# Attention, routed experts and a gated layer on one core: vector arithmetic off GpSimd, another weight decode, Silu, and a written-out plan

## The chip, the core and the metric

One core of a Trainium2 chip runs the whole program in one launch. The metric is the device time in microseconds (us) of that launch, the median of several runs. A core has five engines, each with its own in-order list of instructions: TensorE (PE in the rows; PEld is its weight load), VectorE (DVE), ScalarE (ACT), GpSimd (POOL) and SyncE (SP), which here only issues DMAs. The engines work side by side and wait for each other through semaphores.

## The reference

Three layers on float32 data, the last layer's weights being float64:

```python
# attention: B=4, H=8, S=768, D=48, a state of 48x48 per batch and head
k_n = k / (norm(k) + 1e-6)
for t in range(S):
    y[t]  = q[t] @ state
    v_old = state.T @ k_n[t]
    state = state + beta[t] * outer(k_n[t], v[t] - v_old)
# experts: x is [3072, 384]; tokens with x @ w_skip > 0 go to one of 8 experts
e = argmax(x @ w_gate); gate = softmax(x @ w_gate)[e]
x = x + gate * (relu(x @ w1[e]) @ w2[e])           # w1 384x1024, w2 1024x384
# gated layer
xn  = x / sqrt(mean(x*x) + 1e-6) * rms_g
g   = xn @ w_gate2;  val = xn @ w_val               # 384x1536 each
out = (g * sigmoid(g) * val) @ w_out                # 1536x384
```

## The kernel before

Every float32 product is made of three float16 products: both sides are split into a rounded half "hi" and the rest "lo", and hi.hi, lo.hi and hi.lo are added up in PSUM (`mm3`, lines 296 to 298). So nearly every tensor has a conversion to hi (`conv`, lines 269 to 271, on VectorE or ScalarE) and a subtraction for lo (`tt`, line 277, or `stt`, line 279).

**Attention** runs in six groups g of 128 tokens, each of two halves (chunks of 64 tokens) and of two pairs of batches. For a group: the K tiles are loaded, squared and summed (`norms`), scaled (`kn`), split (`kh`, `kl`), transposed by DMA (`trk`), and multiplied with themselves (`gramk`); the grams go to DRAM and come back with one 32x32 block on each partition (`lda`). `solve` inverts 128 such triangular blocks at once on VectorE: 30 steps, each a multiply (`sm`) and an add (`sa`) of j x (31-j) elements, 60 instructions that depend on each other. Its result is scaled by a mask (`bm`, `Ts`), split in two orders (`Th`, `Tl`), stored, loaded again; `merge` joins 32-blocks to 64-blocks. `prepq` makes the masked q-k products (`pm`, split to `ph`, `pl`), and `step` runs the recurrence of one chunk. Each finished tile is routed (`Route`) and scattered to its expert's rows by indirect DMAs on GpSimd (line 645).

**Experts.** Eight experts one after the other: weights loaded and split (`wh`, `wl`), 256 rows loaded, split, transposed, 64 matmul groups `m1` with relu and lo halves (`relu`, `hl`), then `m2` and a store. Beside them 27 pieces of the gated layer's float64 weights are **decoded** to float32 and split (lines 700 to 709). The buffers of this stage lie over those of attention's that are used up.

**Gated layer.** Groups of 1, 1, 2, 4, 4, 4, 4, 4 tiles of 128 tokens: load, gather the expert's result by an indirect DMA on GpSimd (line 764), add, norm (`sq2`, the root with one Newton step), scale by 1/rms and by rms_g (`xn`), split, transpose; then 12 column blocks of two products `gv`, sigmoid (line 793), times g (`silu`), times val (`gh`), split (`ghh`, `ghl`); then `mo` (lines 804 to 806), copy and store.

**The order.** The kernel does not emit these operations in program order. `Sched.op` records each with the engines that may do it and an estimated cost; `balance` and the tables ORDER, ENGINES and URGENT choose engines and priorities by (stage, tag, group); `run` plays the program through with these costs and picks slots; `emit` writes the lists. In ENGINES a number says how many operations of a tag go to the last engine that may do them: for `kl` 8, 0, 8, 2, 8, 7 of 8 in the six groups on GpSimd, for `kn` 2, 4, 4, 1, 4, 0 of 4, for `pl` 8 of 8, for `gbl` all, for `Ts` in three groups, for `decl` 8, 9, 9 of 9 and for `decm` 9, 6, 8 of 9; `bm` has GpSimd alone. All DMAs but the indirect ones go through SP's list.

## Time and profile before

| | before |
|---|---|
| runs, us | 1086.28, 1085.55, 1086.11 (median 1086.11) |
| profiled execution, span from first to last instruction | 1071.0 us |
| median of the runs less that span | 15.1 us |
| busy in the span: TensorE, VectorE, ScalarE, GpSimd | 821.9, 767.7, 444.5, 298.9 us |
| instructions: VectorE, ScalarE, GpSimd | 1558, 818, 257 |
| mean granted TensorE clock | 0.870 of 2.4 GHz |

Of the profiled execution the page gives the span; what lies around it (launch and end) is in the runs' times alone. A group of instructions in the profile is named by the line of the helper that emitted it, so `kl`, `pl`, `sm` and many others all stand at line 277 and are told apart by engine and shape. "busy" is the union of a group's instructions, "mean" that of one instruction; consecutive instructions of an engine overlap a little in the records. An engine's idle time is put down to what released it last.

### The profile page before, as it was taken

How to read it: one execution, taken by the hardware profiler on the slowest of the kernel's cores; microseconds unless marked ns; L12 is line 12 of the kernel's file. 1: busy time of each engine (PE TensorE's matmuls, PEld its weight loads, DVE VectorE, ACT ScalarE, POOL GpSimd, SP SyncE). 2: the span in 40 equal slices, each digit the busy share in tenths (PEclk: the TensorE clock that was granted, in tenths of full speed). 3: DMA queues.
4: the chain of work that ended last, by engine and by line, in shares of the span. 5: the costliest groups of instructions: out<-in, count | busy, mean ns of one | idle time of the engine just before them, and what ended most of it. 6: DMA issues, size and time to landing. Idle time of an engine off the chain costs nothing. (4 is left out here: it accounts for less than half of the span.)

```text
span 1071.0 us, 23370 instructions
## 1 busy us (share of the span) xinstructions
PE 821.9 (77%) x9590; PEld 568.3 (53%) x9590; DVE 767.7 (72%) x1558; ACT 444.5 (42%) x818; POOL 298.9 (28%) x257
## 2 busy tenths in 40 slices
PE   0440776867667677279898629999999999999996
PEld 0440665756656566267566329754554445445463
DVE  6697998989888888999999999877505651441500
ACT  2230674856657586254535134555202321221200
POOL 7540354335354334421331454330000000000000
PEclk9665687768869697589999859999999999999999
DMA  6985779797998869589776362460210110000000
GB/s 222 212 180 90 165 168 166 209 159 166 187 160 203 165 147 268 186 221 304 217 228 218 127 170 74 119 155 8 37 38 1 30 30 16 15 1 30 1 31 32
DMA packets 307619, 137.94 MB, mean 129 GB/s; under 512 B 273022, under 2 KB 289107, under 8 KB 307506
## 3 DMA queue, kind: packets, MB, share of 16 engines
q1 hardware_dynamic: 304434, 129.32, 50.1%
q0 software_dynamic: 3072, 7.07, 2.3%
q8 instruction: 77, 1.26, 0.5%
q14 instruction: 36, 0.29, 0.1%
HBM read 77.38 MB, written 33.03 MB: 103 GB/s over the span
## 5 line engine op out<-in xcount | busy, mean ns | idle before, releaser
L296 PE MATMUL bank<-arena 128*128 128x64 f16 (+5 forms) x2096 | 381.0, 243 | 158.9 <-DMA arena<-arena 107.3
L277 POOL TENSOR_TENSOR arena<-arena 64x512 f16<-64x512 f32 (+9 forms) x175 | 229.5, 1316 | 574.4 <-ACT arena L269 356.5
L297 PE MATMUL bank<-arena 128*128 128x64 f16 (+5 forms) x2096 | 380.7, 243 | 4.1 <-DVE arena L279 2.1
L298 PE MATMUL bank<-arena 128*128 128x64 f16 (+5 forms) x2096 | 380.0, 243 | 2.1 <-ACT arena L269 2.0
L277 DVE TENSOR_TENSOR arena<-arena 128x512 f16<-128x512 f32 (+22 forms) x503 | 261.1, 523 | 74.6 <-ACT arena L269 59.5
L269 ACT ACTIVATE arena<-arena 128x512 f16<-128x512 f32 (+8 forms) x272 | 194.2, 723 | 239.0 <-DVE arena L279 101.4
L296 PEld LDWEIGHTS <-arena 128*128 128x128 f16 x2096 | 204.9, 105 | 151.7 <-DMA arena<-arena 55.8
L297 PEld LDWEIGHTS <-arena 128*128 128x128 f16 x2096 | 203.7, 104 | 120.5 <-issue 68.6
L269 ACT ACTIVATE arena<-bank 128x384 f16<-128x384 f32 (+4 forms) x286 | 142.2, 520 | 217.2 <-PE bank L806 105.6
L298 PEld LDWEIGHTS <-arena 128*128 128x128 f16 x2096 | 203.6, 104 | 45.9
L279 DVE SCALAR_TENSOR_TENSOR arena<-arena 128x768 f16<-128x768 f32 (+3 forms) x160 | 145.0, 926 | 8.6 <-ACT arena L269 3.5
L277 DVE TENSOR_TENSOR arena<-bank,arena 128x512 f32<-128x512 f32 (+2 forms) x120 | 68.0, 578 | 55.0 <-ACT arena L793 52.5
L806 PE MATMUL bank<-arena 128*128 128x384 f16 x288 | 93.9, 326 | 0.0
L804 PE MATMUL bank<-arena 128*128 128x384 f16 x288 | 93.9, 326 | 0.0
L805 PE MATMUL bank<-arena 128*128 128x384 f16 x288 | 93.9, 326 | 0.0
L279 DVE SCALAR_TENSOR_TENSOR arena<-arena,bank 128x512 f32<-128x512 f32 (+2 forms) x96 | 51.9, 547 | 45.0 <-PE bank L298 44.9
L793 ACT ACTIVATE arena<-bank 128x512 f32<-128x512 f32 (+2 forms) x96 | 45.1, 486 | 74.9 <-PE bank L298 74.6
L747 PE MATMUL bank<-arena 128*128 128x384 f16 x128 | 43.6, 340 | 11.3 <-ACT arena L269 6.1
L270 DVE CAST arena<-arena 64x384 f16<-64x384 f32 (+6 forms) x64 | 33.9, 533 | 21.6 <-PE bank L805 10.7
L302 PE MATMUL bank<-arena 128*128 128x48 f16 x544 | 43.3, 196 | 5.5 <-ACT arena L269 3.8
L306 PE MATMUL bank<-arena 128*128 128x48 f16 x544 | 27.5, 194 | 25.1 <-DVE arena L279 24.2
L749 PE MATMUL bank<-arena 128*128 128x384 f16 x128 | 43.6, 340 | 1.1 <-DVE arena L279 1.1
(107 smaller groups left out, 859.4 us busy)
## 6 DMA issues: line engine op xcount, KB each, us to landing
arena<-in_w_dram SPq DMA_DIRECT2D x24, 512.0 KB, 7.8
arena<-in_w_dram SPq DMA_DIRECT2D x32, 384.0 KB, 4.7
arena<-in_qv_dram SPq DMA_DIRECT2D x12, 768.0 KB, 5.3
gd<-arena SPq DMA_DIRECT2D x12, 512.0 KB, 2.8
arena<-in_kn_dram SPq DMA_DIRECT2D x12, 384.0 KB, 4.3
arena<-gd SPq DMA_DIRECT2D x36, 128.0 KB, 3.1
xd<-arena SPq DMA_DIRECT2D x12, 384.0 KB, 2.9
arena<-in_wg_dram SPq DMA_DIRECT2D x9, 512.0 KB, 4.8
```

The lines of the kernel that those rows point to most:

```text
L269: if e is s.nc.scalar: e.activation(out(),in_(),AF.Copy,scale=scale)
L277: return s.sch.op(alts,lambda e: e.tensor_tensor(out(),a(),b(),op=op),r=r,w=w,tag=tag,prio=prio)
L279: return s.sch.op([("DVE",0.07+n*0.00104)],lambda e: e.scalar_tensor_tensor(out(),a(),sc() if callable(sc) else sc,b(),op0=op0,op1=op1),r= ...
L296: nc.tensor.matmul(out,lh,rh,start=first,stop=False,skip_group_check=True)
L297: nc.tensor.matmul(out,ll,rh,start=False,stop=False,skip_group_check=True)
L298: nc.tensor.matmul(out,lh,rl,start=False,stop=last,skip_group_check=True)
L747: nc.tensor.matmul(py.ap,hT.ap[:,f,0,bs],w.ap[:,0,c],start=f==0,stop=False)
L749: nc.tensor.matmul(py.ap,hT.ap[:,f,1,bs],w.ap[:,0,c],start=False,stop=f==7)
L793: s.act(lambda e,sg=sg,pp=pp: e.activation(sg.ap,pp[0].ap,AF.Sigmoid,scale=2.0**-7),T,[pp[0]],[sg],table="sig",tag="sig")
L804: nc.tensor.matmul(po.ap,hT.ap[:,f,0,bs],s.wo.ap[:,0,c],start=f==0,stop=False)
L805: nc.tensor.matmul(po.ap,hT.ap[:,f,0,bs],s.wo.ap[:,1,c],start=False,stop=False)
L806: nc.tensor.matmul(po.ap,hT.ap[:,f,1,bs],s.wo.ap[:,0,c],start=False,stop=f==11)
```

## The change

- GpSimd keeps the constants, six clears of buffers, and the 48 indirect DMAs. Every `tensor_tensor` goes to VectorE, and so does `bm`.
- The decode clamps the float64 exponent by a maximum (`LEAST`) where it multiplied with a mask; the multiply is gone.
- rms_g is one number for each row of w_gate and w_val. It multiplies the hi and lo halves in the decode (`scale=g`), the normalised tokens lose their scaling by it, and the split of x takes 1/rms as its scale directly, so that `xn` and its buffer are gone.
- ScalarE's Silu takes the place of Sigmoid; the multiply by g is gone.
- ORDER, ENGINES, URGENT and the code that plays the program through are gone. A plan stands in the file instead: the order of all 3630 operations, the engine of each (a digit) and the slot of each of 1627 buffers; `follow` reads it. By its digits VectorE gets 1608 operations, ScalarE 755, GpSimd 66. 24 of the 27 decode pieces are ahead of the first `x2` in VectorE's list; of 48 `kh` 36 are on ScalarE; of 24 `gs` 7 are on VectorE.

The comments are taken out too. The number of slots in each pool stays, but for the decode's temporaries (four for six).

```diff
-    def tt(s,out,a,b,op,n,r,w,engs="DP",tag="",prio=0.0):
-        alts=[]
-        if "D" in engs: alts.append(("DVE",0.07+n*0.00104))
-        if "P" in engs: alts.append(("POOL",0.13+n*0.00194))
+    def tt(s,out,a,b,op,n,r,w,port=1,tag="",prio=0.0):
+        alts=[("DVE",0.07+n*0.00104,port)]
...
+    def follow(s,plan):
+        order,engines,slots=plan
+        for o,e in zip(s.ops,engines): o.eng=ENGINES[int(e)]; o.start=o.end=0.0
+        for b,i in zip(s.bufs,slots): b.slot=i
+        s.order=[s.ops[i] for i in order]
...
-        s.tt(lambda: bm.ap,lambda: s.c.m32.ap,lambda: btg().unsqueeze(2).to_broadcast([128,32,32]),ALU.mult,1024,[bt,s.c.m32],[bm],engs="P")
+        s.tt(lambda: bm.ap,lambda: s.c.m32.ap,lambda: btg().unsqueeze(2).to_broadcast([128,32,32]),ALU.mult,1024,[bt,s.c.m32],[bm])
...
-                t=s.pdt.buf([512],U32); u=s.pdt.buf([512],U32); m=s.pdt.buf([512],F32)
+                t=s.pdt.buf([512],U32); u=s.pdt.buf([512],U32)
+                rs=[] if sc else [s.rg]; g=(lambda sc=sc: sc) if sc else (lambda j=j: s.rg.ap[:,j//3:j//3+1])
                 D(lambda e,t=t,lo=lo: e.tensor_scalar(t.ap,lo(),29,None,op0=ALU.logical_shift_right),[raw],[t],0.34)
-                D(lambda e,t=t,u=u,hi=hi: e.scalar_tensor_tensor(u.ap,hi(),3,t.ap,op0=ALU.logical_shift_left,op1=ALU.bitwise_or),[raw,t],[u])
+                D(lambda e,u=u,hi=hi: e.tensor_scalar(u.ap,hi(),0x7FFFFFFF,None,op0=ALU.bitwise_and),[raw],[u],0.34)
+                D(lambda e,u=u: e.tensor_scalar(u.ap.bitcast(F32),u.ap.bitcast(F32),LEAST,None,op0=ALU.max),[u],[u],0.34)
+                D(lambda e,t=t,u=u: e.scalar_tensor_tensor(u.ap,u.ap,3,t.ap,op0=ALU.logical_shift_left,op1=ALU.bitwise_or),[u,t],[u])
                 D(lambda e,t=t,hi=hi: e.tensor_scalar(t.ap,hi(),0xC0000000,None,op0=ALU.bitwise_and),[raw],[t],0.34)
                 D(lambda e,t=t,u=u: e.scalar_tensor_tensor(u.ap,u.ap,0x3FFFFFFF,t.ap,op0=ALU.bitwise_and,op1=ALU.bitwise_or),[u,t],[u])
-                D(lambda e,t=t,hi=hi: e.tensor_scalar(t.ap,hi(),0x7FFFFFFF,None,op0=ALU.bitwise_and),[raw],[t],0.34)
-                D(lambda e,t=t,m=m,sc=sc: e.tensor_scalar(m.ap,t.ap.bitcast(F32),2.0**-15,sc,op0=ALU.is_ge,op1=ALU.mult),[t],[m],0.34)
-                s.tt(lambda m=m: m.ap,lambda u=u: u.ap.bitcast(F32),lambda m=m: m.ap,ALU.mult,512,[u,m],[m],tag="decm")
-                s.conv(lambda dst=dst,cs=cs: dst.ap[:,0,cs],lambda m=m: m.ap,512,[m],[(dst,(j,0))],tag="dech")
-                s.tt(lambda dst=dst,cs=cs: dst.ap[:,1,cs],lambda m=m: m.ap,lambda dst=dst,cs=cs: dst.ap[:,0,cs],ALU.subtract,512,[m,(dst,(j,0))],[(dst,(j,1))],tag="decl")
+                s.conv(lambda dst=dst,cs=cs: dst.ap[:,0,cs],lambda u=u: u.ap.bitcast(F32),512,[u]+rs,[(dst,(j,0))],scale=g,tag="dech")
+                s.stt(lambda dst=dst,cs=cs: dst.ap[:,1,cs],lambda u=u: u.ap.bitcast(F32),g,lambda dst=dst,cs=cs: dst.ap[:,0,cs],ALU.subtract,512,[u,(dst,(j,0))]+rs,[(dst,(j,1))],tag="decl")
...
-                s.stt(lambda xn=xn: xn.ap,lambda x=x,b=b: x.ap[:,b],lambda ri=ri,b=b: ri.ap[:,b:b+1],lambda: s.rg.ap,ALU.mult,DM,[(x,b),ri,s.rg],[xn],tag="xn")
-                s.conv(lambda xh=xh: xh.ap[:,0],lambda xn=xn: xn.ap,DM,[xn],[(xh,0)],scale=8.0,tag="xnh")
+                s.conv(lambda xh=xh: xh.ap[:,0],lambda x=x,b=b: x.ap[:,b],DM,[(x,b),ri],[(xh,0)],scale=rb,tag="xnh")
...
-                s.act(lambda e,sg=sg,pp=pp: e.activation(sg.ap,pp[0].ap,AF.Sigmoid,scale=2.0**-7),T,[pp[0]],[sg],table="sig",tag="sig")
-                s.tt(lambda sg=sg: sg.ap,lambda pp=pp: pp[0].ap,lambda sg=sg: sg.ap,ALU.mult,T,[pp[0],sg],[sg],engs="D",tag="silu")
+                s.act(lambda e,sg=sg,pp=pp: e.activation(sg.ap,pp[0].ap,AF.Silu,scale=2.0**-7),T,[pp[0]],[sg],table="silu",tag="silu")
...
-        sch.order_by,sch.engines,sch.urgent=ORDER,ENGINES,URGENT
-        sch.run(verbose)
+        sch.follow(PLAN)
```

## Rows read from the trace of the kernel before

**Rows 1.** The windows: length, busy time (instructions) of each engine, clock, DMA share, GB/s.
```profile
0.00:100.00 100.00, 25.68 (x504) 24.84 (x504) 73.13 (x133) 23.62 (x34) 47.73 (x59) 0.73 0.73 178
...
200.00:300.00 100.00, 67.06 (x1567) 60.85 (x1565) 91.09 (x218) 63.86 (x107) 44.63 (x35) 0.79 0.89 175
...
0.00:440.00 440.00, 263.45 (x6033) 234.99 (x6034) 371.12 (x818) 241.77 (x410) 192.77 (x166) 0.76 0.82 180
440.00:612.00 172.00, 134.48 (x965) 96.11 (x965) 167.37 (x270) 72.33 (x134) 54.33 (x40) 0.90 0.72 217
612.00:637.00 25.00, 0.91 (x9) 0.91 (x9) 23.86 (x49) 7.25 (x17) 15.04 (x13) 0.58 0.56 158
637.00:707.00 70.00, 68.67 (x750) 56.91 (x749) 61.60 (x179) 36.51 (x106) 29.43 (x33) 0.98 0.52 124
707.00:1062.00 355.00, 354.41 (x1837) 179.37 (x1834) 143.78 (x246) 86.29 (x154) 7.37 (x7) 1.00 0.09 25
...
```

**Rows 2.** The page's costliest groups: GpSimd, line 277, all forms together.
```profile
...
L277 POOL TENSOR_TENSOR arena<-arena 64x512 f16<-64x512 f32 (+9 forms) x175 | 229.5, 1316 | 574.4 <-ACT arena L269 356.5
...
```

**Rows 3.** Groups by shape, VectorE, whole span: count | busy us, mean ns | idle.
```profile
...
L279 DVE SCALAR_TENSOR_TENSOR arena<-arena 128x768 f16<-128x768 f32 x64 | 67.8, 1067 | 3.6 <-ACT arena L269 3.5
...
L277 DVE TENSOR_TENSOR arena<-bank,arena 128x512 f32<-128x512 f32 x84 | 57.2, 687 | 52.3 <-ACT arena L793 49.9 <-PE bank L298 1.1 <-POOL arena L277 0.8
...
L277 DVE TENSOR_TENSOR arena<-arena 128x512 f16<-128x512 f32 x59 | 40.3, 690 | 59.4 <-ACT arena L269 59.0
...
L279 DVE SCALAR_TENSOR_TENSOR arena<-bank,arena 128x256 f16<-128x256 f32 x64 | 25.3, 413 | 0.0
...
L277 DVE TENSOR_TENSOR arena<-arena 128x220 f32<-128x220 f32 x24 | 14.6, 610 | 0.6
...
L277 DVE TENSOR_TENSOR arena<-arena 64x384 f16<-64x384 f32 x15 | 9.0, 598 | 0.3
...
L277 DVE TENSOR_TENSOR arena<-arena 128x84 f32<-128x84 f32 x24 | 8.3, 346 | 0.6
...
```

**Rows 4.** Groups by shape, VectorE, 564.2 to 583 us, while GpSimd computes nothing.
```profile
...
L279 DVE SCALAR_TENSOR_TENSOR arena<-arena 128x768 f16<-128x768 f32 x8 | 7.5, 948 | 0.0
...
L702 DVE SCALAR_TENSOR_TENSOR arena<-arena 128x512 uint32<-128x512 uint32 x1 | 0.7, 684 | 0.0
...
L703 DVE TENSOR_SCALAR arena<-arena 128x512 uint32<-128x512 uint32 x1 | 0.4, 427 | 0.0
...
```

**Rows 5.** Groups by shape, VectorE, 440 to 612 us, the experts.
```profile
...
L702 DVE SCALAR_TENSOR_TENSOR arena<-arena 128x512 uint32<-128x512 uint32 x21 | 24.9, 1185 | 0.5
...
```

**Rows 6.** Groups by shape, VectorE, 90.2 to 108.9 us, while GpSimd computes nothing.
```profile
...
L277 DVE TENSOR_TENSOR arena<-arena 128x1024 f32<-128x1024 f32 x1 | 1.2, 1224 | 4.8 <-DMA arena<-gd 4.8
...
L277 DVE TENSOR_TENSOR arena<-arena 128x84 f32<-128x84 f32 x2 | 0.5, 246 | 0.1
...
L277 DVE TENSOR_TENSOR arena<-arena 128x220 f32<-128x220 f32 x1 | 0.4, 372 | 0.0
...
```

**Rows 7.** The timeline of VectorE: start us, us together, instruction, xcount.
```profile
...
477.26 2.07 DVE L279 SCALAR_TENSOR_TENSOR arena<-bank,arena 128x256 f16<-128x256 f32 x6
...
```

**Rows 8.** The waits of VectorE, 0 to 612 us: total us, times, longest us.
```profile
...
DVE arena L270 <- POOL arena L277: 6.7, 4, 2.5
...
```

**Rows 9.** The waits of the DMA queue on SP, 0 to 440 us.
```profile
...
SPq L290 <- POOL arena L277: 36.5, 11, 9.0
...
SPq L291 <- POOL arena L277: 10.4, 8, 2.2
...
```

**Rows 10.** Groups by shape, GpSimd, whole span.
```profile
...
L277 POOL TENSOR_TENSOR arena<-arena 64x512 f16<-64x512 f32 x48 | 68.7, 1431 | 66.1 <-ACT arena L269 43.7 <-DVE arena L270 11.5 <-DVE arena L600 4.6
...
L764 POOL DMA_INDIRECT arena<-yd,arena x24 | 26.7, 1112 | 29.9 <-DVE arena L279 23.9 <-issue 3.7 <-DVE arena L769 1.2
L645 POOL DMA_INDIRECT xs<-arena x24 | 26.3, 1095 | 47.0 <-DVE arena L277 19.7 <-DVE arena L271 13.0 <-DVE arena L706 7.4
...
```

More of the change, by code (lines that the diff above doesn't have):

```diff
@@ L44, in __init__ @@
     def __init__(s,pool,shape,dt,name=""):
[L45 removed]
+        s.pool=pool; s.shape=list(shape); s.dt=dt; s.slot=None; s.wr={}; s.rd={}; s.name=name; s._ap=None; s.num=len(pool.sch.bufs); pool.sch.bufs.append(s)
     @property
@@ L56, with __init__ @@
 class Fixed:
-    def __init__(s,ap): s.ap=ap; s.pool=None; s.wr={}; s.rd={}; s.ops=0; s.left=0
+    def __init__(s,ap): s.ap=ap; s.pool=None; s.wr={}; s.rd={}
 class Op:
-    __slots__=("alts","preds","succ","n","prio","ready","bufs","opens","seq","start","end","eng","fn","kind","nb","table","tag","np","late","phase","grp","loc","urg")
-SAME=dict(DVE=0.13,ACT=0.14,POOL=0.1,PE=0.0,SP=2.0)
-LAT=dict(ACT=0.16,DVE=0.14,PE=0.25,POOL=0.1,SP=0.06)
+    __slots__=("alts","preds","seq","start","end","eng","fn","kind","nb","table","tag","late","phase","grp","bufs")
+ENGINES=("PE","DVE","ACT","POOL","SP")
 class Sched:
     def __init__(s,nc,arena,banks):
-        s.nc=nc; s.arena=arena; s.banks=banks; s.pools=[]; s.ops=[]
-        s.boost=0.0; s.phase=0; s.grp=0; s.trace=None; s.order_by={}; s.engines={}; s.urgent={}
+        s.nc=nc; s.arena=arena; s.banks=banks; s.pools=[]; s.ops=[]; s.bufs=[]
+        s.phase=0; s.grp=0; s.trace=None
     def op(s,alts,fn,r=(),w=(),also=(),kind="c",nb=0,table=None,tag="",prio=0.0):
         o=Op(); o.alts=alts if isinstance(alts,list) else [alts]; o.fn=fn; o.kind=kind; o.nb=nb; o.table=table; o.tag=tag
-        o.phase=s.phase; o.grp=s.grp; o.loc=0.0; o.urg=0.0; o.preds=set(); o.succ=[]; o.seq=len(s.ops); o.late=prio+s.boost; bufs={}
+        o.phase=s.phase; o.grp=s.grp; o.preds=set(); o.seq=len(s.ops); o.late=prio; bufs={}
         for x in r:
@@ L92, in op @@
         o.bufs=[b for b in bufs.values() if b.pool is not None]
-        for b in o.bufs: b.left+=1
         o.preds.discard(o)
```

295 lines of the change are left out of this document (77 added, 218 removed), and 76 rows, old and new, of tables (ORDER_, SLOT_).

## The prediction, made before the result was known

> **What bounds the kernel now.** Read the windows first [rows 1]. They cut the span at what the kernel does: attention (0 to 440), experts (440 to 612), a gap in which the first gated group is gathered and normalised (612 to 637), the three small gated groups (637 to 707), the five groups of four tiles (707 to 1062), the last output. In the last two long stretches TensorE is busy 68.7 of 70 and 354.4 of 355 us at a granted clock of 0.98 and 1.00, the 2.4 GHz level: whatever the change does to vector work there, the same matmuls remain. In the first two, VectorE is busy 371.1 of 440 and 167.4 of 172 us, while TensorE has 263.5 and 134.5 and ScalarE 241.8 and 72.3. So what ends last before 612 is VectorE's list, and after 637 TensorE's. A gain must come from the first 637 us.
>
> Then ask what VectorE's busy time is made of. GpSimd's line 277 ran 175 tensor_tensors, 229.5 us [rows 2]. Beside them VectorE's instructions have two durations. The 768-wide scalar_tensor_tensor averages 1067 ns, in a stretch where GpSimd computes nothing 948; the decode's line 702, while the experts run, 1185 against 684 [rows 3, 4, 5]. The solver's multiply and add pairs average 610 (220 wide) and 346 (84 wide), quiet 372 and 246 [rows 3, 6]. A form that reads PSUM is not stretched at all: 413 over the span [rows 3]. So the two engines exclude each other where both use SBUF, and part of VectorE's "busy" is waiting for GpSimd.
>
> How much? The fifteen solver sizes (24 instructions each, 14.6 to 8.3 us a group [rows 3]) sum to 160 us; at quiet durations 119, so 41. The 64 of 768 give 64 x 0.119 = 7.6, the 21 of line 702 among the experts 21 x 0.501 = 10.5: 59 from rows alone. Taking every form against its own median without GpSimd arithmetic, 332 instructions were stretched, by 120 us in all: 78 before 440, 31 from 440 to 612, the rest later. Bounds: 59 from below, GpSimd's whole 229.5 from above; I take 78 and 31.
>
> **Part 1: GpSimd's arithmetic goes to VectorE.** In attention 48 `pl` (64x512), 33 `kl` (64x384), and by the old ENGINES table 15 `kn`, 6 `gbl`, 6 `bm`, 3 `Ts` move. Prices: `pl` as the 690 ns of 128x512, `kl` 0.60, `kn` 0.60 (as `kl`), the fifteen 1024-wide 1.22 [rows 3, 6]: 33.1 + 19.8 + 9.0 + 18.3 = 80 us. Back to back an instruction costs less than its row says: six PSUM halves of 413 take 2.07 us together, so each but the first costs 0.33, 0.08 less [rows 3, 7]. That takes 111 x 0.08 = 9 off. VectorE in attention: 371 - 78 + 80 - 9 = 364. On work alone moving everything wins only 7 us: what GpSimd did costs VectorE about what GpSimd's presence cost it.
>
> The rest is idle time, 440 - 371 = 69. VectorE itself waited 6.7 us for line 277 of GpSimd [rows 8], and 27 of the 69 fall in the first 100 us [rows 1], a start-up that the change keeps in kind. More telling is the DMA queue: SP's transposes waited 36.5 us for GpSimd's lo halves and its other DMAs 10.4 [rows 9]. A lo half of 64x512 takes GpSimd 1.43 us [rows 10], VectorE 0.69: on each of the 24 K tiles the transposed keys can be ready sooner. Against it, the halves now stand in VectorE's own list, behind solver steps. The new order decides which; no row shows it. Bounds for the idle time: 25 (start-up only) to 117 (8 us more in each of six groups). I take 46: 23 off for the waits on GpSimd, under half of the 53.6 us counted. Attention: 364 + 46 = 410, **30 saved**.
>
> **Part 2: decode.** Before, a piece of 512 words took four tensor_scalars (quiet 0.42) and two scalar_tensor_tensors (quiet 0.68) [rows 4], 3.04 us, then a multiply and a lo half, which the ENGINES table put on GpSimd 23 and 26 times of 27. After: four and two again, 3.04, no multiply, and the lo half on VectorE, 0.69 - 0.08 = 0.61. From 440 to 612: -31 for stretching, +19 x 0.61 = +12, and by the new list 24 of 27 pieces precede the first gathered token, where one had begun before 440 and 21 from there to 612 [rows 5]: +2 x 3.7 = +8 (rounded up). VectorE: 167 - 31 + 12 + 8 = 156, with the 5 us of idle 161, **11 saved**. TensorE's 134.5 at a granted clock of 0.90 stays below that.
>
> **Part 3: the first gap.** From 612 to 637 VectorE is busy 23.9 and GpSimd 15.0 of 25 us [rows 1]: the chain gather, add, square, root, scale, split, transpose runs between decode pieces that are stretched. One scaling per tile goes, and the stretching: 25 to 20, **5 saved**; bounds 0 and 10.
>
> **Part 4: Silu and the folded rms_g.** In the gated groups 60 + 12 + 24 multiplies of sigmoid by g go (687 ns each at 512 wide [rows 3]), and 24 scalings by rms_g. ScalarE's Silu replaces its Sigmoid one for one; no row has a Silu, and I price it as the Sigmoid, with the same number of switches to the root and back. All this lies where TensorE is busy 423 of 425 us: **2 saved**, at most 2. If Silu took twice as long, ScalarE's 86 of 355 us would still hide it. The cover is gone only in a small group's first column block, under 1 us.
>
> **Sum.** 30 + 11 + 5 + 2 = 48. The profiled span goes from 1071.0 to 1023. The shown runs have a median of 1086.11 (1085.55 to 1086.28), 15.1 us more than the span, which lie around it and which I take as unchanged: **forecast 1038.** The plan also deals the conversions anew: ScalarE gets 36 of the 48 `kh` (28 before), VectorE 7 of the 24 `gs` (none before). Eight given away and seven taken about cancel, 5 us either way at the outside, and I leave them out; ScalarE has 198 us free in attention.
>
> Against this speaks a rule of the Trainium skill. First the rows: the 48 indirect DMAs that stay on GpSimd took 1112 and 1095 ns [rows 10], in stretches where VectorE was busy 84 to 95% of the time [rows 1]. SBUF — State Buffer (two separate sides, the box on the "DVE blocks DMA" trap) says that a VectorE instruction in its two-port mode keeps GpSimd from writing descriptors, and gives 620 ns alone, about 3100 beside it; by that denser VectorE work would delay these DMAs. By it the four such DMAs that stand on the path would cost an estimated 4 x 2.5 = 10 us. The rows disagree so far, since VectorE was dense already.
>
> **Rivals.**
> 1. *The DMA engines hold attention.* Their share is 0.82 over 0 to 440 [rows 1], which is 361 us of work that the change leaves alone. At a share of 0.89, the most that a hundred microseconds showed (200 to 300), attention takes 405, just under my 410; if the queues give no more than 0.85, it takes 425 and the time is 1086 - 15 - 18 = 1053; at 0.82 nothing is won in attention, 1068. For it: the transposes and the small packets. Against it: VectorE was the busier engine.
> 2. *The order closes the idle time.* Idle 25 would give attention 389, which the DMA bound lifts to 405; the experts come down to TensorE's work there, 134.5 x 0.90 = 121 us at full clock, plus some two thirds of the 37.5 us that it idles, 145, 27 saved; the gap 10. That is 35 + 27 + 10 + 2 = 74 saved, and 16 more if the queues beat 0.89: 996 to 1012.
> 3. *Slower: halves behind solver steps.* VectorE executes its list in order. Where a `kl` stands behind a solver step that waits for a DMA, the transpose, the gram and TensorE wait too, which beside a GpSimd that did it they did not. Price: idle time. With 18 us saved elsewhere it decides from 440 + 18 - 364 = 94 us of idle in attention, 4 us more in each of the six groups than now. At 110 the time is 1102, at the bound of 117 it is 1109.
> 4. *The change does not do what it says:* the long VectorE instructions are long for another reason, such as late operands. Then 109 us stay and 80 - 9 + 12 + 8 come on top of them: about 1177. Against it: unstretched PSUM forms in the same stretches.
> 5. *Descriptors starve.* Two scatters after the last router, two gathers before the first gated group stand on the path. If each waited for two of VectorE's 768-wide instructions, 4 x 1.9 = 8 us: 1046. The rule of SBUF — State Buffer named above would bring this.
>
> **How the numbers follow.** Forecast, 1022 to 1053: 0.48. Rival 1: 0.15. Rival 2: 0.20. Rival 3: 0.09. Rival 4: 0.02. Rival 5: 0.04, inside the forecast's own band. Within 0.2%, about what a measurement of this kernel can tell from no change: 0.02. Range: down to 990, the far end of rival 2 with 0.06 left below, and up to 1073, past rival 1, which leaves the slower cases and the unchanged one out. Faster 0.86, same 0.03, slower 0.11, rivals 3 and 4 holding the last.
>
> **What would show it.** Right: no line 277 on GpSimd; the 768 form at 0.95 and line 702's successors at 0.42 and 0.68 over the span, not only in quiet stretches; VectorE about 520 us busy before the first gated matmul, that one at about 591 instead of 637; from there to the end the same 430 us. Wrong: forms still stretched (rival 4); attention over 430 with a DMA share at 0.82 (rival 1), or with VectorE idle over 94 us and SP waiting on its `kl` (rival 3); a gated part longer than 430, where Silu or its tables would be the cause.

## The result and the profile after

| | before | after |
|---|---|---|
| runs of the first comparison, us | 1086.28, 1085.55, 1086.11, 1087.84 (median 1086.19) | 1076.13, 1077.49, 1076.69, 1075.10 (median 1076.41) |
| ratio, 95% interval | | 0.9912 (0.9894 to 0.9930) |
| span of each of those runs | not on record | 1074.4, 1075.7, 1075.0, 1073.4 |

After is faster by 0.9% here, 9.8 us, where 48 were forecast, and lies above the range (1073). Before's own time differs from chip to chip: 1086 here, 1075 to 1078 on three other chips, 1088 on a fifth. After, run twice more on one of the three, gave 0.9972 (0.9951 to 0.9993) and 0.9988 (0.9968 to 1.0008). Its own time hardly moved (1076.4 here, 1075.5 and 1075.9 there): what differs between these ratios is before. So a ratio below stands for its own chip, and on the fifth chip it holds some 11 us that before takes longer there; where kernels ran on different chips, they are compared by the marks in their traces.

The windows of after, cut at its own stages (columns as in [rows 1]):

```profile
0.00:100.00 100.00, 25.07 (x504) 24.42 (x504) 74.13 (x155) 28.14 (x40) 12.08 (x31) 0.74 0.72 171
200.00:300.00 100.00, 66.89 (x1533) 59.01 (x1529) 81.13 (x202) 68.14 (x113) 3.89 (x4) 0.80 0.85 179
0.00:457.00 457.00, 267.57 (x6033) 237.01 (x6034) 360.63 (x911) 262.20 (x435) 32.81 (x52) 0.74 0.83 174
457.00:620.00 163.00, 129.86 (x965) 95.54 (x965) 150.78 (x303) 67.87 (x125) 4.65 (x4) 0.89 0.78 229
620.00:641.00 21.00, 1.98 (x19) 1.97 (x19) 18.02 (x49) 6.84 (x16) 7.20 (x7) 0.61 0.72 202
...
701.00:1065.00 364.00, 364.00 (x1889) 184.59 (x1886) 111.88 (x197) 74.85 (x135) 5.41 (x5) 1.00 0.11 27
...
```

Read the third line against its like in [rows 1]. VectorE's work fell from 371 to 361 us, as the sum had it (364); attention became 17 us longer all the same. VectorE stood idle for 96 us of 457 where it had 69 of 440 and the forecast 46. From 200 to 300 us it was busy for 81 where it had been for 91.

Groups by shape of after, VectorE, whole span (the answers to [rows 3 to 6]):

```profile
...
L137 DVE SCALAR_TENSOR_TENSOR arena<-arena 128x768 f16<-128x768 f32 x64 | 62.4, 990 | 16.8 <-ACT arena L129 16.6
...
L135 DVE TENSOR_TENSOR arena<-arena 64x512 f16<-64x512 f32 x48 | 32.8, 683 | 3.5 <-ACT arena L129 2.8
L135 DVE TENSOR_TENSOR arena<-arena 64x384 f16<-64x384 f32 x48 | 26.3, 552 | 5.6 <-ACT arena L129 4.5
L137 DVE SCALAR_TENSOR_TENSOR arena<-bank,arena 128x256 f16<-128x256 f32 x64 | 25.1, 417 | 0.2 <-ACT arena L599 0.2
...
L568 DVE SCALAR_TENSOR_TENSOR arena<-arena 128x512 uint32<-128x512 uint32 x27 | 18.4, 684 | 0.1
...
L135 DVE TENSOR_TENSOR arena<-arena 128x220 f32<-128x220 f32 x24 | 9.2, 385 | 0.5
...
```

With GpSimd's arithmetic gone, each form has its quiet duration over the whole span: 684 for the decode's (1185 beside GpSimd), 385 for the solver's 220 (610), and the PSUM form unmoved at 417 (413). The second and third line are the moved halves, 683 and 552 ns against GpSimd's 1431 for the first [rows 10].

The waits of VectorE and of SP's queue in after, 0 to 457 us (total us, times, longest; the answers to [rows 8, 9]):

```profile
DVE arena L135 <- ACT arena L129: 21.7, 22, 5.1
DVE arena L135 <- DMA arena<-gd: 14.3, 2, 8.6
DVE arena L459 <- PE bank L457: 13.3, 12, 2.4
...
```

```profile
SPq L150 <- DVE arena L135: 52.4, 24, 11.9
SPq L150 <- ACT arena L129: 23.9, 15, 3.7
...
SPq L149 <- DVE arena L135: 14.7, 10, 3.3
...
```

VectorE's list now waits for ScalarE's conversions (line 129), for the grams' way through DRAM (`gd`), and in front of copies of nine logits (line 459), which take 0.17 us each. SP's waits for GpSimd have become waits for VectorE's line 135. None of these sums says by itself what holds the end: a wait can go and the end stay, as a_conv shows below.

The same marks in seven profiled executions, us from the start of the span, read from the trace as the first or last instruction of the kind named (the kernels are those of the next section):

| | before | b0_again | after | a_third | b_swap | b_fold | b_fold_wide |
|---|---|---|---|---|---|---|---|
| last logit copy (attention) | 438.0 | 437.7 | 455.6 | 460.0 | 439.9 | 431.8 | 420.0 |
| first relu of the experts | 462.9 | 460.8 | 485.9 | 489.9 | 462.4 | 453.9 | 442.5 |
| last `m2` | 610.4 | 611.4 | 619.4 | 618.4 | 605.5 | 591.7 | 581.7 |
| first Sigmoid or Silu | 637.5 | 639.1 | 641.9 | 642.0 | 629.4 | 614.3 | 604.4 |
| last `mo` | 1061.5 | 1065.0 | 1064.7 | 1064.7 | 1053.1 | 1035.3 | 1025.6 |
| span | 1071.0 | 1074.7 | 1074.4 | 1074.3 | 1062.2 | 1045.0 | 1035.1 |

### The profile page after: what moved, and what is told of

The parts are those of the page before. It is cut to its first block, busy times and chain, and to the rows that moved or that the text cites. A ratio compares the mean times of both kernels' runs of the same rounds, so it can differ in the third digit from the quotient of the medians.

```text
span 1074.4 us, 23128 instructions
## 1 busy us (share of the span) xinstructions
PE 820.8 (76%) x9590; PEld 569.4 (53%) x9590; DVE 686.5 (64%) x1610; ACT 447.6 (42%) x800; POOL 63.4 (6%) x79
## 5 line engine op out<-in xcount | busy, mean ns | idle before, releaser
L135 DVE TENSOR_TENSOR arena<-arena 128x150 f32<-128x150 f32 (+24 forms) x624 | 288.6, 472 | 105.4 <-ACT arena L129 75.7
L155 PEld LDWEIGHTS <-arena 128*128 128x128 f16 x2096 | 204.9, 105 | 158.7 <-DMA arena<-arena 65.7
L129 ACT ACTIVATE arena<-arena 128x768 f16<-128x768 f32 (+9 forms) x257 | 195.7, 776 | 184.0 <-DVE arena L137 49.3
L156 PEld LDWEIGHTS <-arena 128*128 128x128 f16 x2096 | 203.4, 104 | 110.0 <-issue 61.5
L157 PEld LDWEIGHTS <-arena 128*128 128x128 f16 x2096 | 203.4, 104 | 46.1 <-issue 0.3
L137 DVE SCALAR_TENSOR_TENSOR arena<-arena 128x768 f16<-128x768 f32 (+4 forms) x163 | 138.9, 869 | 31.2 <-ACT arena L129 23.2
L662 PE MATMUL bank<-arena 128*128 128x384 f16 x288 | 93.9, 326 | 0.0
L663 PE MATMUL bank<-arena 128*128 128x384 f16 x288 | 93.9, 326 | 0.0
L664 PE MATMUL bank<-arena 128*128 128x384 f16 x288 | 93.9, 326 | 0.0
L161 PE MATMUL bank<-arena 128*128 128x48 f16 x544 | 41.5, 194 | 16.2 <-issue 7.6
L130 DVE CAST arena<-arena 128x512 f16<-128x512 f32 (+5 forms) x81 | 30.0, 373 | 35.5 <-PE bank L663 32.7
L504 POOL DMA_INDIRECT xs<-arena x24 | 25.4, 1058 | 430.1 <-DVE arena L135 250.7
L607 PE MATMUL bank<-arena 128*128 128x384 f16 x128 | 42.3, 330 | 5.3 <-DVE arena L131 5.3
L162 PEld LDWEIGHTS <-arena 128*128 128x128 f16 x544 | 35.7, 104 | 18.2 <-issue 15.4
L624 POOL DMA_INDIRECT arena<-yd,arena x24 | 26.0, 1082 | 289.7 <-ACT arena L129 154.7
L162 PE MATMUL bank<-arena 128*128 128x48 f16 x544 | 41.2, 194 | 1.6 <-ACT arena L129 1.1
```

Of the source, the lines that this page charges most:

```text
L129: if e is s.nc.scalar: e.activation(out(),in_(),AF.Copy,scale=sc)
L135: return s.sch.op(alts,lambda e: e.tensor_tensor(out(),a(),b(),op=op),r=r,w=w,tag=tag,prio=prio)
L137: return s.sch.op([("DVE",0.07+n*0.00104,port)],lambda e: e.scalar_tensor_tensor(out(),a(),sc() if callable(sc) else sc,b(),op0=op0,op1=op ...
L155: nc.tensor.matmul(out,lh,rh,start=first,stop=False,skip_group_check=True)
L156: nc.tensor.matmul(out,ll,rh,start=False,stop=False,skip_group_check=True)
L157: nc.tensor.matmul(out,lh,rl,start=False,stop=last,skip_group_check=True)
```

## The experiments

The question is who keeps VectorE idle in attention. The theories: **V**, VectorE's amount of work is still the bound; **L**, the low halves wait in its list (rival 3); **C**, conversions moved to ScalarE make it wait; **D**, the transfers hold attention (rival 1), and **Q**, SyncE's one queue does; **O** or **P**, the new plan (order, engines, slots) does. Beside these **M**, what the 15.1 us around the span are.

**Before again.** No edit.

> The kernel before, unchanged, for its span in timed executions. After: the four executions' times lie 1.7 to 1.8 us above their spans. The forecast took the 15.1 us between before's profiled span (1071.0) and its median (1086.1) as something that stays. Theory M (the profiled execution of before was a shorter one than those that were timed): spans of about 1084.4 here, 1.7 us under the times, and the true gain in span is then 1084.4 - 1074.7 = 10 us, not -3. Rival M2 (before has 15 us of work outside of its span, which the change took away): spans of about 1071 beside times of 1086, and then all of the measured gain of 9.8 us lies outside the span.

Measured: spans 1070.7 to 1079.5 beside times of 1072.45 to 1081.16, in each of the ten runs 1.7 to 1.8 apart. M holds: nothing of 15 us lies around the span. The execution that [rows 1] come from was 13.4 us shorter than the timed runs that were shown with it (1086.1 less 1.7 and less 1071.0); it is like the runs on the three chips, and whether it ran on the chip of those timed runs is not on record. The window of attention, for what follows:

```profile
0.00:438.00 438.00, 263.98 (x6033) 235.31 (x6034) 367.39 (x807) 241.60 (x409) 191.09 (x165) 0.74 0.84 180
```

In before, b0_again, b_gate and b_wide attention ends at 437.5 to 438.0. In three profiled executions of after it ends at 455.6, 460.0 and 462.3, so a difference of 7 us from one execution of after's kind is not clear of noise.

**The parts behind attention alone** (`b_gate`), in before's planner:

```diff
-e.activation(sg.ap,pp[0].ap,AF.Sigmoid,scale=2.0**-7)
+e.activation(sg.ap,pp[0].ap,AF.Silu,scale=2.0**-7)
...
-s.tt(lambda m=m: m.ap,lambda u=u: u.ap.bitcast(F32),lambda m=m: m.ap,ALU.mult,512,[u,m],[m],tag="decm")
```

> Before, with the change's parts behind attention alone: ScalarE's Silu, rms_g folded into the gate and value weights, the other float64 decode. GpSimd keeps its arithmetic in attention and in the decode's low halves that it still has; the order comes from before's planner. What the forecast gave these parts: the gap 5 us, the gated part 2 us, and of the experts' 11 us the decode's shorter list. So 1086 - 7 to -13: 1073 to 1079 if these parts alone carry the gain that was measured (then attention's rework brought nothing on the whole); 1080 to 1086 if they hide behind the matmuls and the gain of 9.8 us comes from VectorE being rid of the shared port. Attention itself (last logit copy at 438 us) should stay within some 5 us, since nothing of it is changed but what the planner fills in.

Measured: 1092.2 us, ratio 1.0167 (1.0139 to 1.0194). Attention as before (437.5), but the experts took 174.9 us from first relu to last `m2` (150.6 in b0_again). With other operations the planner, whose numbers were set for the old ones, dealt another order. That this order cost the 24 us is the likely reading and not shown; the run does not price the parts.

**After's engines in another order** (`b_both_on`): after's operations and engine digits, order and slots from before's planner.

```diff
+        for o,e in zip(ops,ON_):
+            o.alts=[x for x in s.full[o.seq] if x[0]==('PE','DVE','ACT','POOL','SP')[int(e)]]
```

> After's operations, each on the engine on which after has it, but with order and slots from before's planner, whose order numbers were set for the old work. Attention in after: VectorE 361 us busy, 96 us idle, end at 457. Theory O (the idle time is the written order's doing: in VectorE's list stand copies of logits, halves of the off-diagonal block and the like right where their input comes late): another order has its waits elsewhere; the 14 us before the logit copies, 14 before the low halves of that block and 7 before a gram copy go away or change by more than 10 us, with busy time the same within 5 us. Theory C (the idle time comes with the engines: high halves made on ScalarE, low halves on VectorE, so that each low half waits for the other engine's queue): the same 85 to 105 us idle whatever the order, mostly released by ScalarE's conversions. Theory D (the DMA engines hold attention, 0.91 of them busy from 100 to 200 us): the same end at 457 within 10 us, and waits for the gram blocks, inverses and transposes the same. The order numbers are not fitted to this work, so a longer attention (470 to 520 us, total 1090 to 1140) is what O expects.

Measured: 1121.9 us, 1.0439 (1.0394 to 1.0484); attention ends at 463.6, with VectorE 364 us busy of 464 and idle for 100. A second order over the same engines has the same idle time. O in its narrow form (this order alone) is not borne out, but the order numbers were not fitted. The run decides little: 100 us of idle time is what C expected, 463.6 what D did, and 1121.9 us in all what O did.

**Low halves back on GpSimd** (`a_pool`): in after, the digits of the 96 `kl` and `pl` from VectorE to GpSimd.

> After, with all 96 low halves of K and of the masked gram (kl, pl) put back on GpSimd in attention, at their places in the written order. Takes 48 x 0.55 + 48 x 0.69 = 60 us of work off VectorE (361 to 301), gives GpSimd 96 x about 1.43 = 137 us, and brings back the stretch of VectorE's forms that read and write the State Buffer: at most as much as before's 78 us. Theory L (rival 3 of the forecast: the low halves wait in VectorE's list, and the path pays): attention ends earlier than 457, by 10 to 25 us. Theory O (the order of the other waiting operations): VectorE's busy time comes back to about 360, the waits of the logit copies, the off-diagonal block and the gram copies stay, and attention ends at 457 to 480. Theory D (DMA): the end stays at 457 within 5 us whatever VectorE does.

Measured: 1097.4 us, 1.0219 (1.0184 to 1.0254). Attention ends at 477.7, 15 to 22 us later than in after; VectorE 347 us busy, 131 idle. L in the form that VectorE is the wrong place falls: under this order GpSimd is worse.

**After again** (`a_again`). No edit.

> After, unchanged, beside before on one chip. On another chip before's executions took 1071 to 1081 us with 1.7 us around the span, where the first comparison had 1086 for it and 1076 for after. If the first comparison holds on this chip too: after 0.9% under before. If before's span is what differs from chip to chip: a ratio of 0.995 to 1.005 here, as the two profiled spans (1071.0 and 1074.4) had it. In the profile: attention's last logit copy at 455 +- 3 us, VectorE 361 us busy before 457.

Measured: 1075.5 us, 0.9972 (0.9951 to 0.9993). Attention 462.3.

**Conversions back on VectorE** (`a_conv`): in after, 33 `QT`, 11 `Th` and 6 `gbh` from ScalarE.

> After with the copies of Q (QT, 33 of 44), the high halves of the inverse (Th, 11 of 12) and those of the off-diagonal gram block (gbh, 6) on VectorE instead of ScalarE, at the same places in the order. Takes 33 x 1.05 + 11 x 1.47 + 6 x 1.05 = 57 us off ScalarE (262 to 205 before 457) and gives VectorE 33 x 0.41 + 11 x 1.0 + 6 x 0.7 = 29 us (361 to 390). Theory C (ScalarE's queue holds attention: followed back from its last logit, the path of before runs 234 us on VectorE and 46 on ScalarE, after's 85 and 142): attention ends 10 to 25 us earlier than 457, with some 45 us of idle time on VectorE in place of 96. Theory O (the written order puts waiting operations ahead, whatever engine they wait for): the end within 5 us. Theory V (VectorE's amount of work is the bound): 15 to 29 us later. Theory D (DMA engines): within 5 us.

Measured: 1082.1 us against 1077.7, 1.0041 (1.0014 to 1.0068); attention 468.7, VectorE 382 us busy of 469. VectorE's waits for ScalarE in front of line 135 fell from 26.3 us (a_again) to 6.0, and attention ended later all the same. C falls for these three tags; the `kh` and `ph` that ScalarE makes were not tried.

The path that the expectation quotes (85 us on VectorE, 142 on ScalarE) came from a trace of after in which no transfer's landing could be told, and the traces differ in this (296 of 464 landings in a_again, 42 in b0_again, 24 in b_fold). A walk that needs no landings goes back from the last logit copy by the semaphores: from an instruction to whoever raised the semaphore that it waited for, if that came after the end of the instruction before it on its engine, and otherwise to that instruction. Worked out so from the traces, in us up to the last logit copy:

| on the path | b0_again | b_swap | after | a_again | a_third | b_fold | b_fold_wide |
|---|---|---|---|---|---|---|---|
| VectorE | 202 | 205 | 123 | 104 | 110 | 191 | 235 |
| SyncE's issuing and the transfers | 90 | 90 | 141 | 155 | 158 | 107 | 55 |

In after the path leaves VectorE for the transfers. This is one way to go back, and another gives other sizes; what a part is worth only an experiment tells.

**VectorE relieved, packets relieved** (`s_dve`, `s_dma`), in after, one execution of each:

```diff
-s.tt(lambda o=o: o(1),i,lambda o=o: o(0),ALU.subtract,384,...
+s.tt(lambda o=o: o(1)[:,0:1,0:1],lambda i=i: i()[:,0:1,0:1],lambda o=o: o(0)[:,0:1,0:1],ALU.subtract,384,...
```

```diff
-W.ap[32*b:32*b+32,:,:,:,32*b:32*b+32].rearrange("p q h l c->p (q h l) c"), ... td.ap[b,16*hf:16*hf+16].rearrange("a l r c->r (a l) c")
+W.ap[32*b:32*b+32,:,:,0,32*b:32*b+32].rearrange("p q h c->p (q h) c"), ... td.ap[b,16*hf:16*hf+16,0].rearrange("a r c->r a c")
```

> After with the 96 low halves of K and of the masked gram (kl, pl) made for one element of each row alone, all instructions and waits in place: the rest of the low halves stays zero, so this leaves out part of the precision. VectorE is rid of 96 x about 0.55 = 53 us in attention (361 to 308). Theory V (VectorE's amount): attention ends 40 to 53 us earlier, near 405 to 415. Theories C, O, D (queues of others, the order, DMA): VectorE's idle time takes most of it up, and the end moves by 5 to 20 us.

> After where the loads of the inverse (wz, dn, W) and of the off-diagonal block (GB) bring the high halves alone, which leaves out the low halves: some 61,000 of the 307,000 packets are gone, all in attention, with the same number of transfers, waits and issues. Theory D (the DMA engines, busy for 0.83 of attention and 0.91 from 100 to 200 us, hold it): their share falls to 0.7 and attention ends 20 to 50 us earlier than 457. Theories C and O: 0 to 10 us earlier, by what those transfers land sooner.

The windows of s_dve and then of s_dma, to the end of attention:

```profile
0.00:456.00 456.00, 269.25 (x6033) 238.75 (x6034) 318.41 (x909) 262.01 (x434) 33.09 (x51) 0.74 0.83 174
```

```profile
0.00:438.00 438.00, 264.75 (x6033) 235.33 (x6034) 359.19 (x904) 262.59 (x434) 33.90 (x51) 0.75 0.77 172
```

42 us off VectorE move attention's end by 0 to 7 us (455.6 to 462.3 in after, here 455.4; the run 1071.8): the rest became idle time, 138 of 456. The smaller loads move it by 18 to 24 (to 437.8; the run 1055.6), with VectorE's work unchanged. V falls; the path of after runs through the transfers. These loads lost packets and bytes together, and SyncE's issuing fell with them, from 293 us in a_again to 257; s_dma does not tell the three apart.

**The same two reliefs in before** (`b_sdve`, `b_sdma`), and **both in after** (`s_two`), again one execution of each.

> Before with its 96 low halves of K and of the masked gram made for one element of each row alone (81 of them on GpSimd), order and waits as they are: leaves out the low halves. GpSimd is rid of most of its arithmetic in attention, VectorE of the stretch that this brings and of 15 short operations. The step of the forecast that this tries: 78 us of stretch go, and attention follows VectorE. Theory V (VectorE holds before's attention, so that its work comes off the end): the last logit copy moves from 438 to 380 or 395. Theory D (behind VectorE, as near as this, stand the transfers and SyncE's one queue): it stops at 415 to 430 and VectorE's idle time grows by 40 us or more.

> Before with the edit of s_dma: the loads of the inverse and of the off-diagonal block bring the high halves alone (leaves out the low halves; 61,000 packets fewer in attention). In after this took 20 us off the run and brought attention's last logit copy from 462 to 438. Theory V+D (before is held by VectorE, after by the transfers): here 0 to 8 us. Theory D alone (both are held by the transfers): 20 us or more here too.

> After with both reliefs, the low halves' operations of kl and pl made for one element (53 us off VectorE) and the loads without their low halves (61,000 packets fewer): leaves out the low halves. Alone they moved the last logit copy from 462 to 455 and to 438. If the transfers are a bound by themselves, with VectorE next behind it: together more than the sum of 31 us, 40 to 60 (402 to 422). If the chain runs in turn through all of them and each is worth its own share: the sum, 425 to 435.

The windows of b_sdve and then of b_sdma:

```profile
0.00:418.00 418.00, 256.75 (x6033) 229.69 (x6034) 311.26 (x801) 240.79 (x409) 112.53 (x165) 0.76 0.90 189
```

```profile
0.00:428.00 428.00, 260.72 (x6033) 233.52 (x6034) 368.40 (x803) 241.53 (x409) 192.03 (x165) 0.76 0.75 175
```

Before answers the other way round: 20 us for VectorE's relief (437.7 to 418.2; run 1055.8), 10 for the packets' (428.1; run 1066.2). Even there 56 us less of busy VectorE (with it 79 less of GpSimd, which made 81 of these halves) bring only 20, and the DMA share rises to 0.90. In after both together bring 22 to 28 (433.8; run 1053.6) where alone they bring 18 to 31 in sum: not the 40 to 60 of a bound with VectorE next behind it. That the chain goes through each in turn is the reading that is left, within this noise.

**A second issuer** (`a_q2`): in after, the 60 `ldk`, `ldq`, `xd`, `gout` and `td` issued by GpSimd.

> After with 60 of the transfers of attention (loads of K and of Q and V, writes of grams, inverses and outputs: 128 rows each) issued by GpSimd, which has 33 us to do in attention, instead of by SyncE; packets and bytes as before. SyncE's queue: 293 us of issuing in 462, of which these are 32 us, and it no longer stands before a write whose input is late (td on VectorE's low halves, gout on the gram copies, xd on the outputs). Theory Q (SyncE's one queue, its issuing and its waits in order, holds attention): 10 to 25 us earlier. Theory D (the DMA engines' packets hold it, whoever issues): within 5 us. Against both: GpSimd's issues wait for VectorE's port, and loads come later: 5 to 20 us later.

Measured: 1101.3 us, 1.0225 (1.0176 to 1.0273); attention 480.7. Q in this form falls: without the 60, SyncE still issues for 287 us (293 in a_again), since a transpose takes it 3.8 us on average instead of 3.3. Why is not settled.

**Before's plan with VectorE in GpSimd's place** (`b_swap`): the change's first part alone. The old planner still counts with GpSimd; then each of its 175 operations is emitted on VectorE at the same place.

```diff
+        for o in sch.ops:
+            if o.eng=="POOL" and o.kind=="c" and o.tag in TOV: o.eng="DVE"
```

> Before with its own order and slots, but GpSimd's 175 operations on VectorE at the same places of the order: the change's first part alone. VectorE in attention: 371 us less 78 of stretch plus 80 moved, 364 to 373. Theory P (the new order and the moved conversions cost after's attention its 18 to 24 us): attention ends at 430 to 445 here. Theory L (the low halves in VectorE's list make K's and P's halves late, in whatever order): 455 to 480. What comes after attention: decode's low halves and products on VectorE, experts 5 to 15 us longer than before's.

Measured: 1064.5 us against 1088.4, **0.9781 (0.9767 to 0.9795)**. This is the fifth chip; against b0_again's span, 1074.7, the 1062.2 of b_swap are 12.5 us less, not 24. The window to the end of attention:

```profile
0.00:440.00 440.00, 265.48 (x6033) 234.61 (x6034) 366.15 (x916) 241.71 (x409) 36.53 (x54) 0.77 0.83 179
```

VectorE's work is 366 us where after has 361, idle 74 instead of 96 to 102. The halves stand in VectorE's list here too, so they do not cost the 18 to 24 us in whatever order; their places in the new order remain a part of the plan. P holds: what after lost in attention came with the new plan.

Attention is no shorter than in before, though nothing waits for GpSimd's arithmetic any more. SP's waits for tensor_tensors, the low halves among them, show why: first b0_again, 0 to 438 us, then b_swap, 0 to 440 (line 290 issues the transposes, line 291 the other transfers):

```profile
SPq L290 <- POOL arena L277: 43.6, 12, 8.4
SPq L291 <- DVE arena L277: 31.3, 17, 11.7
...
SPq L290 <- DVE arena L277: 11.3, 7, 3.1
...
SPq L291 <- POOL arena L277: 8.2, 7, 2.0
...
```

```profile
SPq L290 <- DVE arena L277: 44.6, 13, 15.2
SPq L291 <- DVE arena L277: 40.9, 22, 11.6
...
```

In sum 94 us became 86. That one half takes VectorE 0.69 us and GpSimd 1.43 hardly shows in it.

**All of the change's arithmetic in before's plan** (`b_fold`), and **after a third time** on the same chip:

```diff
-s.tt(lambda sg=sg: sg.ap,lambda pp=pp: pp[0].ap,lambda sg=sg: sg.ap,ALU.mult,T,[pp[0],sg],[sg],engs="D",tag="silu")
+s.sch.op([("DVE",0.07+T*0.00104)],lambda e: None,r=[pp[0],sg],w=[sg],tag="silu")
```

> After, unchanged, a third time, to stand on the same chip beside the two kernels below. 0.988 to 1.000 of before, as on the two chips so far (0.9912 and 0.9972).

> All of the change's arithmetic (no operation of GpSimd but scatters, gathers and constants; the other decode; rms_g in the weights; Silu) in before's order and slots: dropped operations leave their place empty, moved ones keep it; the norm keeps one product of x and the factor of a token. Theory P (the new plan cost after what its arithmetic brought): attention ends at 437 to 443, VectorE in the experts 27 x 0.69 = 19 us less than in b_swap, so 5 to 15 us off its 143 us, the gap 2 to 4 us shorter: a profiled span of 1040 to 1055, a ratio of 0.965 to 0.975. Against it (the forecast's sum was too large in the experts and the gap too): no faster than b_swap's 0.978.

Measured: a_third 1075.9 us, 0.9988 (0.9968 to 1.0008); b_fold 1046.8 us, **0.9723 (0.9700 to 0.9746)**, both beside 1077.05. The windows of b_fold, and under them that of a_third:

```profile
100.00:200.00 100.00, 67.14 (x1642) 59.35 (x1643) 85.96 (x219) 61.97 (x109) 4.10 (x4) 0.77 0.96 173
200.00:300.00 100.00, 69.10 (x1625) 61.76 (x1621) 90.06 (x251) 65.07 (x109) 7.13 (x7) 0.76 1.00 181
...
0.00:432.00 432.00, 258.88 (x6033) 230.52 (x6034) 367.80 (x919) 241.30 (x409) 37.27 (x54) 0.78 0.90 182
...
```

```profile
0.00:460.00 460.00, 272.14 (x6033) 241.38 (x6034) 360.01 (x904) 262.46 (x434) 32.85 (x51) 0.73 0.84 172
...
```

And the waits of VectorE in attention, first a_third, then b_fold (line 459 there is 602 here, 457 is 600):

```profile
DVE arena L135 <- ACT arena L129: 26.2, 24, 5.8
DVE arena L135 <- DMA arena<-gd: 14.2, 2, 8.6
DVE arena L459 <- PE bank L457: 13.6, 15, 1.9
DVE arena L137 <- ACT arena L129: 11.2, 11, 6.1
...
```

```profile
DVE arena L338 <- ACT arena L337: 15.5, 4, 5.9
DVE arena L279 <- DMA arena<-gd: 8.2, 3, 6.1
DVE arena L279 <- ACT arena L271: 7.9, 6, 2.7
...
DVE arena L602 <- PE bank L600: 2.7, 4, 1.0
```

The same arithmetic, 28 us apart in attention and 29 in the span. In the new plan VectorE stands 24 times before a tensor_tensor whose high half ScalarE has not made yet and 15 times before a logit copy, in the old one 6 and 4 times. The path back from the last logit has 191 us on VectorE in b_fold and 110 in a_third, and 107 against 158 in SyncE's issuing and the transfers. SyncE issues no less in b_fold (300 us of 432, against 290 of 460): it is not the amount of issuing that tells the two apart. Attention ends 5 us before the band that was expected, and 8 before b_swap's, though hardly anything but the parts behind attention differs; the two ran on different chips, and the cause is open.

**Wider packets** (`a_wide`, `b_wide`, `b_fold_wide`): high and low half interleaved, so that a load moves 128 bytes a packet instead of 64; nothing is left out.

```diff
-dn=s.pdn.buf([2,H,2,128],F16); W=s.pW.buf([2,H,2,128],F16)
+dn=s.pdn.buf([2,H,128,2],F16); W=s.pW.buf([2,H,128,2],F16)
...
-td.ap[b,16*hf:16*hf+16].rearrange("a l r c->r (a l) c")
+td.ap[b,16*hf:16*hf+16].rearrange("a r c l->r a (c l)")
```

> After, with the high and low halves of the inverse and of the off-diagonal block interleaved element by element (td, tn, wz, dn, W, GB): each packet of these loads is 128 bytes instead of 64, some 61,000 packets fewer in attention, all bytes, operations and the order as before, nothing left out. The stationary matrices of z, x1 and u are then read at every second element, the halves Th, Tl, gbh and gbl written so. Theory D (packets and their issuing hold after's attention; the loads without low halves brought 24 us of attention): 12 to 24 us of attention, the run 1052 to 1064. If it was the bytes, not the packets: within 5 us. Against it: slower conversions and weight loads at a stride of two: up to 10 us back.

> Before with the same interleaving. The loads without low halves brought before 10 us of attention (438 to 428), with VectorE 289 us on its path there. Theory V+D: 0 to 10 us here, less than in after. If both kernels gain the same, the transfers hold both alike.

> b_fold with the high and low halves of the inverse and of the off-diagonal block interleaved, so that these loads move packets of 128 bytes. In after this brought 3 to 10 us of attention, in before none in the profiled executions and 0.8% in the timed ones. If VectorE holds attention in this order: 0 to 4 us. If the transfers stand right behind it: 4 to 10 us.

Measured: a_wide 1071.2 us against 1088.4, 0.9836 (0.9821 to 0.9850), attention 452.6 where after had 455.6 to 462.3, so less than the 12 to 24 expected. Its packets are as many as in s_dma (242,994 on the page) and SyncE issues for 264 us (257 there), so fewer packets and less issuing do not make up s_dma's gain: either the bytes count too, or the interleaving costs something back (ScalarE has 10 us more to do, 272 for 262); no run here separates these. Of the ratio, some 11 us are this chip's slower before: after took 1075.5 to 1076.4 elsewhere, 4 to 5 us more than a_wide. b_wide 1079.3, 0.9918 (0.9901 to 0.9936), attention 438.0, unmoved; its span, 1074.5, is that of b0_again, so the ratio shows no gain of its own. b_fold_wide **1036.3 us, 0.9608 (0.9585 to 0.9631)**, 10 us under b_fold and the fastest here:

```profile
0.00:420.00 420.00, 263.21 (x6033) 234.47 (x6034) 368.54 (x916) 251.15 (x409) 37.15 (x54) 0.76 0.84 188
```

More than the 4 to 10 expected: attention 12 us shorter, VectorE idle for 51, DMA share back at 0.84, and the path 235 us on VectorE and 55 in issuing and transfers.

## Why the prediction was wrong

**The work: right, with some luck.** Stretching gone, halves moved, 9 us off for overlap: 364 us forecast for VectorE in attention, 361 measured in after, 366 and 368 in b_swap and b_fold. After's is the lowest, and there the plan had moved more conversions to ScalarE than the two tags that the prediction counts as cancelling: ScalarE has 262 us for 242, 435 instructions for 410. For the experts 156 forecast, 151 measured. The 768 form came to 0.99, not 0.95.

**The idle time of attention: the step that failed.** "I take 46: 23 off for the waits on GpSimd" had no row, as the prediction says. Measured are 96 to 102 in after, and attention ended at 456 to 462 where 410 was forecast, nearly the whole miss in the span (1074 for 1023). The bounds (25 to 117) held it, the value did not. Two things were wrong in it, of about the same size. First, the waits on GpSimd did not come off. In the old plan with VectorE in GpSimd's place (b_swap) none is left, and VectorE is idle for 74 us (71 in b0_again): SP's waits for halves, 94 us in b0_again, are 86 there, all of them now for VectorE. Work taken off VectorE does not come off the end either: in before itself 56 us less of busy time gave 20 (b_sdve). So the best that the arithmetic reached in the old plan is 432 (b_fold, idle 64), 22 us above the forecast. Second, the plan was taken as something that would bring the idle time down; by the side of b_fold it cost 24 to 30 us more.

**Rival 3** named the price (it decides from 94 us of idle time) and its signs came, idle time above that and SP waiting for VectorE's halves, but not as halves that are late in any order: b_swap has them in VectorE's list and ends attention at 440, and SP's waits for VectorE's tensor_tensors are longer in sum in b_fold (48.2 us in front of transposes, 33.5 in front of other transfers) than in after (14.7 and 52.4).

**Rival 1** came, in another form than the prediction gave it: in the new plan the DMA engines' share is 0.83, no ceiling, yet the path has 141 to 158 us in issuing and transfers, and leaving out half of some loads brings 18 to 24. In the old plan it came nearer once VectorE was relieved: 0.90 in attention, 0.96 and 1.00 in two stretches, and packets of 128 bytes gave 12 us. The 361 us of DMA work that the rival takes as fixed were not: share times length is 379 in after and 389 in b_fold, for the same number of packets over the whole run. DMA: Bandwidth & Descriptors, section "Why small descriptors are slow (HBM only)", in the Trainium skill puts a fixed cost on each packet and on each descriptor; b_fold and b_fold_wide agree in direction, 0.90 x 432 = 389 against 0.84 x 420 = 353 us of DMA time.

**The 15.1 us: misread, without moving the forecast change.** They were taken as lying around the span and unchanged. Each run on record here takes 1.7 to 1.9 more than its span. Since 1071.0 and 15.1 add up to the runs' median, the forecast is that median less 48 with or without the misreading. But a profiled span beside runs of another execution is no difference to read: by the two profiled spans (1071.0 and 1074.4) after was slower, by runs on one chip it is 0.1 to 0.9% faster.

**The other terms.** From the marks, after against before and b_fold against b0_again. Experts 11 us, first relu to last `m2`: 14.0 in after (147.5 to 133.5), 12.8 in b_fold; but between the last logit and the first relu after lost 5 of it (24.9 to 30.3). Gap 5: 4.6 and 5.1. Gated part 2: 1.2 and 4.9; Silu costs what Sigmoid did. Rival 5 did not come: the indirect DMAs of after took what they took in before (1095 and 1112 ns [rows 10]), with VectorE busy for 79% of attention, where the scatters run, and 86% of the gap, where the first gathers do:

```profile
...
L624 POOL DMA_INDIRECT arena<-yd,arena x24 | 26.0, 1082 | 289.7 <-ACT arena L129 154.7 <-DVE arena L137 130.8 <-DVE arena L636 1.2
L504 POOL DMA_INDIRECT xs<-arena x24 | 25.4, 1058 | 430.1 <-DVE arena L135 250.7 <-ACT arena L129 91.2 <-DVE arena L501 58.9
...
```

SBUF — State Buffer, section "A bandwidth-pool intuition that's wrong (but worth ruling out)", in the Trainium skill has a DMA of GpSimd wait for its descriptors beside a tensor_copy of VectorE, about 3100 ns where it takes 620 alone; no run here shows that.

So in the old plan the arithmetic brought 30 of the 48 us that were forecast (b_fold's span, 1074.7 to 1045.0), and the plan took nearly all of it away again. The steps in b_fold: attention 6 for 30, from there to the first relu 1 for none, experts 13 for 11, gap 5 for 5, gated 5 for 2. Behind attention the terms came to their forecast or above it; attention's term failed under either plan.

**Still open:** whether the new plan's order, its choice of engines or its slots cost the 28 us. b_both_on (new engines, other order) and a_conv (new order, 50 conversions back) both kept the loss, but neither stands in an order made for it. TensorE's mean granted clock in attention is 0.73 of 2.4 GHz in a_third and 0.78 in b_fold, and its same 6033 matmuls are busy for 272 and 259 us: whether that is a part of the cause or follows from the waits, no run tells. And why before takes 1075 us on one chip and 1088 on another.

## What to carry to other kernels

When a change brings new work and a new order together, take the order apart from the work: emit the new work at the old places first. Work that is taken off the busiest engine comes off the end only as far as the next holder allows; take some of it away for a look (a narrowed operation, half the packets) before counting on it. And read a span and a time from the same execution, on the same chip, before taking their difference for something.

## What the chip showed that was not expected

Issuing takes SyncE more than half of attention, and a transpose takes it longest. SyncE's timeline in a_third (start, us together, count):

```profile
101.90 6.75 SPq L150 DMA_DIRECT2D arena<-td  x6
...
126.20 6.73 SPq L149 DMA_TRANSPOSE arena<-arena  x2
133.03 0.52 SPq L150 DMA_DIRECT2D arena<-in_qv_dram  x1
133.61 5.97 SPq L149 DMA_TRANSPOSE arena<-arena  x1
```

The first line is two loads of 2048 runs of 64 bytes and four of 1024. In a_third's attention the median issue of a load of 2048 such runs takes 0.96 us, of 1024 runs 0.65, of the 128 rows of Q and V 0.52; single ones range from 0.3 to 3.9. The 36 transposes take 1.6 to 7.8 us, 3.2 on average. Together SyncE issues for 290 of a_third's 460 us.

ScalarE's Silu costs what its Sigmoid did, 596 against 595 ns for 128x512 out of PSUM; each switch between its table and the root's took 1283 ns, seven each way in after and six in before, where the prediction had the same number:

```profile
L652 ACT ACTIVATE arena<-bank 128x512 f32<-128x512 f32 x60 | 35.7, 596 | 131.1 <-PE bank L157 99.0 <-DVE arena L135 22.9 <-DVE arena L137 9.1
...
L652 ACT ACT_TABLE_LOAD x7 | 9.0, 1283 | 0.1
```
